# One exponential over two key chunks in a clustered-attention and channel-mix kernel

## The chip, the cores and the metric

The kernel runs on one core of one Trainium2 chip. The metric is device time in microseconds. The kernel before takes 244.97 us (median of 3 runs, 244.86 to 246.22). The profiled execution has a span of 243.7 us from its first to its last instruction.

## The reference

There are 4 batches, 8 heads, 768 positions and 64 values a head. Every query and key is assigned to one of 16 clusters of its head by the largest product with the cluster's normalized centroid, and a query attends only to keys of its own cluster. The attention output, with its heads side by side (512 values a position), goes through a channel mix. All data is fp32 at the ends.

```python
# attention, for each batch and head
mask   = q_assign[:, :, :, None] == k_assign[:, :, None, :]
scores = scale * np.matmul(q, k.transpose(0, 1, 3, 2))
scores = np.where(mask, scores, -1000000000.0)
scores = scores - np.max(scores, axis=-1, keepdims=True)
attn   = np.exp(scores)
attn   = attn / (np.sum(attn, axis=-1, keepdims=True) + 1e-09)
out    = np.matmul(attn, v)
# channel mix; x_prev is x moved on by one position
xk = mu_k * x + (1.0 - mu_k) * x_prev
xr = mu_r * x + (1.0 - mu_r) * x_prev
k  = np.maximum(xk @ w_k, 0.0)          # 512 -> 1024
v  = k * k @ w_v                        # 1024 -> 512
r  = 1.0 / (1.0 + np.exp(-(xr @ w_r)))  # 512 -> 512
return r * v
```

## The kernel before

The heads go in 16 pairs, four to a batch. Queries and keys are transposed, so that the 64 values lie on partitions, and 16 more rows hold each position's cluster as a one-hot vector. The product over these 80 rows gives the score plus a step for "same cluster", which the exponential's bias and scale turn into the mask. The keys come in 6 chunks of 128 (NCH), the queries in thirds of 256 (QT). A *group* is one third of the queries for the two heads of a pair, so it has 6 steps of scores and exponentials, and 4 blocks of value matmuls. There are 48 groups and 288 steps. A column of ones beside the values gives the sum of the exponentials, by which `norm` divides.

The score tiles lie in PSUM, each one bank of 512 columns (two heads by 256 queries), in a ring of four:

```python
ptp   = ctx.enter_context(tc.tile_pool(name="ptp", bufs=3 * NCH))
ps_st = ctx.enter_context(tc.tile_pool(name="ps_st", bufs=4, space=bass.MemoryType.PSUM))

def scores(t):                                    # TensorE, line 315
    g, c = divmod(t, NCH)
    ...
    st = ps_st.tile([128, 2, QT], F32, name="st")
    for s, (tt, hf) in enumerate(parts):
        ...
        nc.tensor.matmul(st[:, s, :].rearrange("p (r u) -> p r u", r=2), w, x, start=True, stop=True)
    sts[t] = st

def exps(t):                                      # ScalarE, line 321
    pt = ptp.tile([128, 2, QT], BF16, name="pt")
    nc.scalar.activation(pt, sts.pop(t), AF.Exp, bias=-BIG, scale=BIG)
    pts[t] = pt

def values(t):                                    # TensorE, line 333: 6 matmuls of 65 columns a block
    ...
    for c in range(NCH):
        nc.tensor.matmul(o[:, i, :], pts[g * NCH + c][:, s, qc * 128:(qc + 1) * 128],
                         vts[n % NR][:, tt, 2 * (c % 3) + c // 3, 0:D + 1], start=(c == 0), stop=(c == NCH - 1))
```

VectorE divides (lines 343, 348), copies the transposed result, and makes the difference to the position before and the two mixes, one for w_k and one for w_r. The first w_k matmul of a batch needs the mix of all four pairs:

```python
def diff(self, n):                                # VectorE, line 401
    ...
    nc.vector.tensor_tensor(self.d, xcur(n, self.hf), xprev(n, self.hf), op=ALU.subtract)
def lerp(self, n, dst, mu):                       # VectorE, line 405: xk and xr
    ...
    nc.vector.scalar_tensor_tensor(out=..., in0=self.d, scalar=mu[:, j:j + 1], in1=xcur(n, self.hf),
                                   op0=ALU.mult, op1=ALU.add)
```

The channel mix is w_k (line 414) into one bank, a Relu on ScalarE (420), a square on VectorE (424), w_r (430) with a Tanh on ScalarE (435), w_v (463), and a product on VectorE (469). For these accumulators there are three banks of their own (`ps_w`); once all attention is done, the score ring and the output bank serve too:

```python
def psum512(pool):
    if pool == "st":
        return ps_st.tile([128, 512], F32, name="mst", tag="st")
    if pool == "o":
        return ps_o.tile([128, 512], F32, name="mo", tag="out2")
    wslot[0] = int(pool[1])
    return wtile([128, 512], F32, "mw")
```

Before a pair's scores, TensorE transposes q and k of the first pairs (line 163, copied by line 173), multiplies by the centroids (195), and VectorE and a hop through DRAM make the one-hot rows (lines 201 to 225).

The order of the instructions on each engine is set when the program is built. Each piece of work is a task with an estimated length, its dependencies, and the ring slots that it takes and frees. The planner runs through these and picks, for each engine, the task that can start first. Tables push single tasks earlier or later (`URGE`, `HOLD`); `PACE0` and `PACE1` set how many score steps go before each slice of channel mix.

```python
task(("scores", t), "PE", 0.225, lambda t=t: scores(t), deps=need, ..., new=[("st", ("st", t))], rank=0, sub=t)
task(("exp", t), "ACT", 0.48, lambda t=t: exps(t), deps=[("scores", t)], uses=[("st", t)],
     new=[("pt", ("pt", t))], rank=1, sub=t)
```

Of the kernel before, what the change touches and what calls it, by code (L numbers as in the profile page):

```python
# [8 lines left out]
F32 = mybir.dt.float32  # L9
BF16 = mybir.dt.bfloat16  # L10
AF = mybir.ActivationFunctionType
# [5 lines left out]
def kernel(  # L17
# [13 lines left out]
    nc = tc.nc  # L31
# [18 lines left out]
    BIG = 32.0  # L50
# [11 lines left out]
    clup = ctx.enter_context(tc.tile_pool(name="clup", bufs=2))  # L62
    ptp = ctx.enter_context(tc.tile_pool(name="ptp", bufs=3 * NCH))
    xnp = ctx.enter_context(tc.tile_pool(name="xnp", bufs=5))
# [5 lines left out]
    hopp = ctx.enter_context(tc.tile_pool(name="hopp", bufs=3, space=bass.MemoryType.DRAM))  # L70
    ps_st = ctx.enter_context(tc.tile_pool(name="ps_st", bufs=4, space=bass.MemoryType.PSUM))
    ps_o = ctx.enter_context(tc.tile_pool(name="ps_o", bufs=1, space=bass.MemoryType.PSUM))
# [228 lines left out]
    def scores(t):  # L301
        g, c = divmod(t, NCH)
        n, parts = groups[g]
        rows = slice(0, 64 + C)
        st = ps_st.tile([128, 2, QT], F32, name="st")
        for s, (tt, hf) in enumerate(parts):
            a = augs[n % NR]
            w = a[rows, 2 + tt, c // (NCH // 2), :]
            if n < ROWS:
                w = w[:, (c % (NCH // 2)) * 128:(c % (NCH // 2) + 1) * 128]  # L310
            else:
                w = w.rearrange("k (u m) -> k m u", m=NCH // 2)[:, c % (NCH // 2), :]
            x = a[rows, tt, 1, hf * QU:(hf + 1) * QU]
            x = bass.AP(tensor=x.tensor, offset=x.offset, ap=[x.ap[0], [-HS, 2], x.ap[-1]])
            nc.tensor.matmul(st[:, s, :].rearrange("p (r u) -> p r u", r=2),  # L315
                             w, x, start=True, stop=True)
        sts[t] = st

    def exps(t):
        pt = ptp.tile([128, 2, QT], BF16, name="pt")  # L320
        nc.scalar.activation(pt, sts.pop(t), AF.Exp, bias=-BIG, scale=BIG)  # L321
        pts[t] = pt

# [57 lines left out]
    def psum512(pool):  # L381
        if pool == "st":
            return ps_st.tile([128, 512], F32, name="mst", tag="st")
        if pool == "o":
            return ps_o.tile([128, 512], F32, name="mo", tag="out2")
        wslot[0] = int(pool[1])
        return wtile([128, 512], F32, "mw")
# [110 lines left out]

    HOLD = {('aff1', 1): 11.7, ('diff', 0, 0): 34.3, ('load', 3, 0): 10.6, ('norm', 12): 70.5, ('xcp', 3, 2): 69.8}
    URGE = {('aff', 6): -1, ('aff1', 1): -1, ('affb', 1): -1, ('affb', 5): -1, ('cast', 1, 2): -1, ('cast', 6, 0): -1, ('cast', 7, 3): -1, ('diff', 1, 1): -1, ('diff', 2, 1): 2, ('hop1', 5): -1, ('hop2', 3): 4, ('lerpk', 0, 0): -1, ('lerpr', 0, 0): -1, ('load', 4, 0): -1, ('load', 5, 1): -1, ('load', 6, 4): 4, ('load', 7, 2): 4, ('load', 8, 1): 4, ('load', 8, 2): -1, ('load', 8, 4): 4, ('load', 8, 5): -1, ('norm', 1): -1, ('norm', 14): 2, ('norm', 3): -1, ('out', 0, 0, 0): 4, ('psk', 0, 0, 0): -1, ('relu', 0, 0, 3): -1, ('scores', 19): -1, ('scores', 21): -1, ('scores', 22): -1, ('scores', 35): -1, ('scores', 38): -1, ('scores', 45): -1, ('scores', 57): 2, ('scores', 63): 4, ('scores', 66): -1, ('scores', 68): -1, ('scores', 75): 4, ('scores', 77): -1, ('scores', 82): -1, ('scores', 90): -1, ('scores', 94): -1, ('scores', 96): -1, ('tcp', 1, 1): -1, ('tcp', 2, 0): -1, ('tpe', 5, 0): -1, ('vcast', 2): -1, ('vcast', 3): -1, ('wv', 0): 2, ('wv', 6): -1, ('xcp', 1, 2): -1, ('xcp', 2, 2): -1, ('xtr', 1, 2): 2, ('xtr', 2, 0): -1, ('xtr', 3, 2): -1}  # L500
    MARGIN = 0.46
    WK, WR, WV = 20.1, 52.3, 35.9
    ROWS = 6
    PACE0, PACE1 = 115.3, 2.13
    PREP = 7
    LATE = {"load": 2.7, "vload": 2.7, "hop1": 0.6, "hop2": 1.0, "xcp": 1.2}
    TAIL = {"PE": 0.25 + MARGIN, "ACT": 0.2 + MARGIN, "DVE": 0.15 + MARGIN, "POOL": 0.15, "SP": 0.0}

# [115 lines left out]
    with tc.manual_schedule():  # L624
# [18 lines left out]
        def use_pe(m):  # L643
            wps = ps_st.tile([128, 512], F32, name="wps", tag="st")
            for i in range(m):
                nc.tensor.matmul(wps[:, 0:256], warm[:, 0:128], warm, start=True, stop=True)  # L646
# [59 lines left out]
        STEPB = NSTEP // B  # L706
        START = {3: 0, 4: 15, 5: 45, 6: 35, 7: 45}
        for n in range(2 * NP, NPAIR):
            b, j = divmod(n, NP)
            START[n] = STEPB * b - 53 + 15 * j  # L710
        moving = {}
# [22 lines left out]
        for n in range(1, NPAIR):  # L734
# [17 lines left out]
            if n > 0:  # L752
                task(("vload", n), "SP", 0.63, lambda n=n: load_v(n, nc.sync), rank=2, sub=due[n] + 4, step=due[n] - 13,
                     new=[("vnat", ("vnat", n))], behind=[("vload", n - 1)] if n > 1 else [])
                moving["vload", n] = 1.1
# [48 lines left out]
        for t in range(NSTEP):  # L804
            g, c = divmod(t, NCH)
            n, parts = groups[g]
            need = sum((ready(n, tt) for tt in {tt for tt, _ in parts}), []) if c == 0 else []
            task(("scores", t), "PE", 0.225, lambda t=t: scores(t), deps=need, after=0.0 if t else 9.9, behind=[("scores", t - 1)] if t else [],
                 new=[("st", ("st", t))], rank=0, sub=t)
            task(("exp", t), "ACT", 0.48, lambda t=t: exps(t), deps=[("scores", t)], uses=[("st", t)],  # L810
                 new=[("pt", ("pt", t))], rank=1, sub=t)
        for t in range(NVAL):
# [3 lines left out]
                 deps=[("exp", g * NCH + NCH - 1), ("vcast", n)] if i == 0 else [],  # L816
                 uses=[("pt", g * NCH + c) for c in range(NCH)] + ([("o", g)] if i else []),
                 new=[] if i else [("o", ("o", g))], rank=2, sub=t)
# [111 lines left out]
        for i in range(4):  # L930
            task(("wk", i), "POOL", 0.75, lambda i=i: load_wk(i), rank=0, after=WK + 3.9 * i)
            moving["wk", i] = 1.8
# [3 lines left out]
        for i in range(4):  # L936
            task(("wv", 2 * i), "POOL", 0.75, lambda i=i: load_wv(2 * i), rank=2, after=WV + 2.4 * i)
            moving["wv", 2 * i] = 1.8

        rings = {"w0": 1, "w1": 1, "w2": 1, "st": 4, "o": 1, "nat": 4, "vnat": 3, "qkT": 2, "t1": 2, "ohn": 2, "oht": 2, "hop": 3,  # L940
                 "pt": 3 * NCH, "xn": 5, "xk": 6, "xr": 6, "k2": 2, "diff": 3, "kr": 3, "tanh": 3, "out": 3}
        held = {"nat": [("nat", i) for i in range(3)], "vnat": [("vnat", 0)], "qkT": [("qkT", 0)]}
# [29 lines left out]
```

The softmax here doesn't subtract the row's maximum and nothing guards it: scores larger than these inputs give would overflow.

## Time and profile before

| | before |
|---|---|
| time, median of 3 | 244.97 us |
| span of the profiled execution | 243.7 us |
| TensorE busy | 237.6 us |
| ScalarE busy | 193.4 us |
| VectorE busy | 190.1 us |
| GpSimd busy | 90.9 us |
| TensorE clock granted | 0.997 |

PE is TensorE's matmuls, PEld its weight loads, DVE VectorE, ACT ScalarE, POOL GpSimd, SP the engine that issues most transfers. The busy tenths cut the span into 40 slices of 6.1 us. In the groups, the columns are line, engine, operation, output and input, count, busy time in us and mean length in ns, and after the second bar the idle time of the engine just before, with what ended it. A matmul's end is modelled, and consecutive ones overlap in the record. The chain of waits follows the work that ended last back to the start, and cuts each piece to the time that it added. In a timeline the columns are the start, the length of the merged run, the engine and the operation with its count. A row by stretch gives for each engine the busy time and, in brackets, its instructions, and then the granted clock, the transfer share and GB/s.

### The profile page before, as it was taken

Reading aid. Unit: us, or ns where it says so; the run is one execution under the profiler, and the core shown is the slowest. Engines: PE = TensorE matmul, PEld = TensorE weight load, DVE = VectorE, ACT = ScalarE, POOL = GpSimd, SP = SyncE. Lnnn points to the kernel's source line nnn. Section 1 sums busy time; section 2 is a strip of 40 time slices with the busy share of each in tenths; the row PEclk is TensorE's granted clock in tenths of the full one; section 3 lists DMA queues with packets and bytes.
Section 4 is the critical chain, followed back from the end, with each engine's and each line's share of the span. In section 5 each row is a group of like instructions: output and inputs, shape, how many; then the busy total and the mean of one; then the engine's idle time right before and its main releaser. Section 6 shows DMA issues by size and latency. Waiting matters only on the chain.

```text
span 243.7 us, 7114 instructions
## 1 busy us (share of the span) xinstructions
PE 237.6 (98%) x2693; PEld 177.3 (73%) x2693; DVE 190.1 (78%) x496; ACT 193.4 (79%) x370; POOL 90.9 (37%) x183
## 2 busy tenths in 40 slices
PE   8999999999999999999999999999999999999994
PEld 6777885878669677876967767867778769576562
DVE  3498899999988989799879897999648577663232
ACT  5279999999889989998988778989987989442340
POOL 3648959476376153313662615355400000000000
PEclk9999999999999999999999999999999999999998
DMA  6955599999999988569795777672622121122112
GB/s 166 312 176 106 137 234 283 193 142 186 133 227 159 175 158 164 109 157 173 164 177 115 157 103 213 108 182 67 169 74 71 29 65 57 29 83 86 46 44 86
DMA packets 94659, 33.61 MB, mean 138 GB/s; under 512 B 75296, under 2 KB 91168, under 8 KB 94624
## 3 DMA queue, kind: packets, MB, share of 16 engines
q1 hardware_dynamic: 91072, 30.19, 56.4%
q0 software_dynamic: 2208, 2.62, 7.1%
q10 hardware_dynamic: 1344, 0.33, 0.7%
q8 instruction: 21, 0.34, 0.7%
q14 instruction: 14, 0.11, 0.2%
HBM read 25.63 MB, written 7.77 MB: 137 GB/s over the span
## 4 chain that ended last, share of the span: by engine, by line
PE 90%; DVE 7%; ACT 1%; issue 1%; ACTq 0%
PE st L315 24%; PE mw L414 15%; PE mw L463 14%; PE out L333 13%; PE mw L430 6%; PE affps L195 4%; PE mst L414 2%; PE mst L463 2%; PE trps L163 2%; PE wps L646 2%; PE mst L430 2%; PE mo L430 1%; DVE xr L405 1%; DVE xk L405 1%; DVE aug L179 1%; DVE qkT L173 1%
## 5 line engine op out<-in xcount | busy, mean ns | idle before, releaser
L321 ACT ACTIVATE pt<-st 128x512 bf16<-128x512 f32 x288 | 151.5, 640 | 12.6 <-PE st L315 11.5
L179 POOL TENSOR_SCALAR aug<-qkT 64x384 bf16<-64x384 f32 x122 | 65.1, 534 | 72.7 <-DVE qkT L153 42.9
L315 PE MATMUL st<-aug 80*128 80x256 bf16 x576 | 91.4, 272 | 0.7
L315 PEld LDWEIGHTS <-aug 80*128 80x128 bf16 x576 | 52.6, 101 | 24.5 <-issue 10.8
L333 PE MATMUL out<-vt,pt 128*128 128x65 bf16 x1152 | 49.1, 192 | 0.0
L333 PEld LDWEIGHTS <-pt 128*128 128x128 bf16 x1152 | 46.1, 97 | 3.1 <-issue 0.6
L414 PE MATMUL mw<-xk,w_k_sb 128*128 128x256 bf16 x336 | 42.6, 272 | 0.0
L414 PEld LDWEIGHTS <-w_k_sb 128*128 128x128 bf16 x384 | 36.9, 98 | 5.1
L463 PE MATMUL mw<-w_v_sb,k 128*128 128x512 bf16 x160 | 40.4, 378 | 0.0
L424 DVE TENSOR_TENSOR k<-kr 128x512 bf16<-128x512 bf16 x48 | 21.9, 455 | 12.5 <-ACT kr L420 12.3
L420 ACT ACTIVATE kr<-mw 128x512 bf16<-128x512 f32 x42 | 25.7, 611 | 7.2 <-PE mw L414 6.8
L463 PEld LDWEIGHTS <-k 128*128 128x128 bf16 x184 | 17.4, 97 | 14.6
L405 DVE SCALAR_TENSOR_TENSOR xr<-diff,mu_r_sb,xt 128x256 bf16<-128x256 bf16 x48 | 24.9, 536 | 0.0
L405 DVE SCALAR_TENSOR_TENSOR xk<-diff,mu_k_sb,xt 128x256 bf16<-128x256 bf16 x48 | 23.2, 503 | 0.1
L153 DVE STREAM_TRANSPOSE qkT<-qk_nat 128x384 f32<-128x384 f32 x40 | 21.8, 557 | 0.2 <-DMA qk_nat<-in_k_dram 0.2
L186 POOL CAST vt<-v_nat 128x384 bf16<-128x384 f32 x32 | 17.5, 576 | 11.5 <-DMA v_nat<-in_v_dram 10.6
L469 DVE SCALAR_TENSOR_TENSOR out_sb<-tanh,mw 128x512 f32<-128x512 bf16 x20 | 13.5, 674 | 10.1 <-PE mw L463 6.9
L348 DVE TENSOR_TENSOR xn<-out,rs 128x256 bf16<-128x256 f32 x46 | 19.5, 424 | 1.6
L401 DVE TENSOR_TENSOR diff<-xt 128x256 bf16<-128x256 bf16 x48 | 16.0, 333 | 1.1
L430 PE MATMUL mw<-w_r_sb,xr 128*128 128x512 bf16 x64 | 16.4, 378 | 0.0
L430 PEld LDWEIGHTS <-xr 128*128 128x128 bf16 x96 | 9.0, 97 | 7.2
L343 DVE RECIPROCAL rs<-out 128x4 f32<-128x4 f32 x48 | 8.2, 171 | 7.1 <-PE out L333 6.6
(70 smaller groups left out, 178.5 us busy)
## 6 DMA issues: line engine op xcount, KB each, us to landing
v_nat<-in_v_dram SPq DMA_DIRECT2D x16, 384.0 KB, 5.2
out_dram<-out_sb SPq DMA_DIRECT2D x23, 256.0 KB, 2.2
qk_nat<-in_q_dram SPq DMA_DIRECT2D x40, 96.0 KB, 3.4
qk_nat<-in_k_dram SPq DMA_DIRECT2D x40, 96.0 KB, 3.6
qk_rows<-in_q_dram SPq DMA_DIRECT2D x5, 384.0 KB, 5.9
qk_rows<-in_k_dram SPq DMA_DIRECT2D x5, 384.0 KB, 6.6
hop<-oht SPq DMA_DIRECT2D x15, 96.0 KB, 2.3
aug<-hop SPq DMA_DIRECT2D x15, 96.0 KB, 3.6
```

Source lines behind the costliest of these rows:

```text
L153: nc.vector.transpose(qkT[n][:, g, :], nat[n][:, g // 2, (g % 2) * GW:(g % 2 + 1) * GW])
L179: (eng or nc.gpsimd).tensor_scalar(augs[n % NR][0:64, g, par, :], in0=qkT[n][64 * par:64 * par + 64, g, :], scalar1=qk_scale, scalar2=1.0, ...
L315: nc.tensor.matmul(st[:, s, :].rearrange("p (r u) -> p r u", r=2), w, x, start=True, stop=True)
L321: nc.scalar.activation(pt, sts.pop(t), AF.Exp, bias=-BIG, scale=BIG)
L333: nc.tensor.matmul(o[:, i, :], pts[g * NCH + c][:, s, qc * 128:(qc + 1) * 128], vts[n % NR][:, tt, 2 * (c % 3) + c // 3, 0:D + 1], start=( ...
L348: nc.vector.tensor_tensor(x.rearrange("p q t d -> p t q d"), o[:, :, 0:D].rearrange("p (t q) d -> p t q d", t=2), rs.rearrange("p (t q) -> ...
L405: nc.vector.scalar_tensor_tensor(out=dst[:, j, :].rearrange("p (r u) -> p r u", r=2), in0=self.d, scalar=mu[:, j:j + 1], in1=xcur(n, self. ...
L414: nc.tensor.matmul(ps[:, i * QT:(i + 1) * QT], w_k_sb[:, j, (2 * i2 + i) * 128:(2 * i2 + i + 1) * 128], self.xk[:, j, :], start=(j == 0), ...
L420: nc.scalar.activation(self.kr[i2], self.ps.pop(i2), AF.Relu, scale=0.5 ** 0.5)
L424: nc.vector.tensor_tensor(self.k2[:, 2 * i2:2 * i2 + 2, :].rearrange("p i u -> p (i u)"), kr, kr, op=ALU.mult)
L430: nc.tensor.matmul(ps, self.xr[:, j, sl], w_r_sb[:, j, :], start=(j == 0), stop=(j == NJ - 1))
L463: nc.tensor.matmul(self.ps["v", c], self.k2[:, i, sl], w_v_sb[:, i, :], start=(i == 0), stop=(i == NI - 1))
```

## The change

Two steps of scores share a tile of two PSUM banks, and one exponential of 1024 columns takes both. This halves the number of exponentials (144 in place of 288), for less fixed cost on ScalarE. The rings keep their bytes: two score tiles of two banks, 9 exponential tiles of twice the size. A value block reads its half of the tile. Where the score ring serves the channel mix, an accumulator takes the first bank of a tile. The planner has new lengths (0.86 for an exponential), and its tables and constants were searched anew, so the order differs on all engines; among others the w_k and w_v loads are placed closer together, and the loads and preparation of later pairs start at other steps.

```diff
-    ptp = ctx.enter_context(tc.tile_pool(name="ptp", bufs=3 * NCH))
+    ptp = ctx.enter_context(tc.tile_pool(name="ptp", bufs=3 * NCH // 2))
-    ps_st = ctx.enter_context(tc.tile_pool(name="ps_st", bufs=4, space=bass.MemoryType.PSUM))
+    ps_st = ctx.enter_context(tc.tile_pool(name="ps_st", bufs=2, space=bass.MemoryType.PSUM))
@@ scores
-        st = ps_st.tile([128, 2, QT], F32, name="st")
+        if t % 2 == 0:
+            sts[t // 2] = ps_st.tile([128, 2, 2, QT], F32, name="st")
+        st = sts[t // 2][:, t % 2]
...
-        sts[t] = st
@@ exps
-        pt = ptp.tile([128, 2, QT], BF16, name="pt")
-        nc.scalar.activation(pt, sts.pop(t), AF.Exp, bias=-BIG, scale=BIG)
-        pts[t] = pt
+        pt = ptp.tile([128, 2, 2, QT], BF16, name="pt")
+        nc.scalar.activation(pt, sts.pop(t // 2), AF.Exp, bias=-BIG, scale=BIG)
+        pts[t - 1], pts[t] = pt[:, 0], pt[:, 1]
@@ psum512
-            return ps_st.tile([128, 512], F32, name="mst", tag="st")
+            return ps_st.tile([128, 2, 512], F32, name="mst", tag="st")[:, 0]
@@ the planner's constants (HOLD and URGE, some 90 entries, left out)
-    MARGIN = 0.46
+    MARGIN = 0.19
-    PACE0, PACE1 = 115.3, 2.13
-    PREP = 7
-    LATE = {"load": 2.7, "vload": 2.7, "hop1": 0.6, "hop2": 1.0, "xcp": 1.2}
+    PACE0, PACE1 = 107.6, 2.16
+    PREP = 13
+    LATE = {"load": 2.7, "vload": 2.7, "hop1": 0.0, "hop2": 1.0, "xcp": 1.2}
@@ when later pairs may be loaded
-        START = {3: 0, 4: 15, 5: 45, 6: 35, 7: 45}
+        START = {3: 0, 4: 15, 5: 45, 6: 50, 7: 52}
-            START[n] = STEPB * b - 53 + 15 * j
+            START[n] = STEPB * b - 75 + 14 * j
@@ tasks
             task(("scores", t), "PE", 0.225, ...
-                 new=[("st", ("st", t))], rank=0, sub=t)
-            task(("exp", t), "ACT", 0.48, lambda t=t: exps(t), deps=[("scores", t)], uses=[("st", t)],
-                 new=[("pt", ("pt", t))], rank=1, sub=t)
+                 new=[] if t % 2 else [("st", ("st", t + 1))], uses=[("st", t)] if t % 2 else [], rank=0, sub=t)
+            if t % 2:
+                task(("exp", t), "ACT", 0.86, lambda t=t: exps(t), deps=[("scores", t - 1), ("scores", t)], uses=[("st", t)],
+                     new=[("pt", ("pt", t))], rank=1, sub=t)
@@ weight loads
-            task(("wk", i), "POOL", 0.75, lambda i=i: load_wk(i), rank=0, after=WK + 3.9 * i)
+            task(("wk", i), "POOL", 0.75, lambda i=i: load_wk(i), rank=0, after=WK + 1.7 * i)
-            task(("wv", 2 * i), "POOL", 0.75, lambda i=i: load_wv(2 * i), rank=2, after=WV + 2.4 * i)
+            task(("wv", 2 * i), "POOL", 0.75, lambda i=i: load_wv(2 * i), rank=2, after=WV + 1.3 * i)
@@ rings
-        rings = {..., "st": 4, ..., "pt": 3 * NCH, ...}
+        rings = {..., "st": 2, ..., "pt": 3 * NCH // 2, ...}
```

## The prediction

> **What bounds the kernel now.** I read the page's busy shares first, then the busy tenths, then the groups by line, the chain of waits in order of time, and last the timelines of ScalarE and VectorE in the stage where the chain leaves TensorE.
>
> ```profile
> PE 237.6 (98%) x2693; PEld 177.3 (73%) x2693; DVE 190.1 (78%) x496; ACT 193.4 (79%) x370; POOL 90.9 (37%) x183
> ...
> PE   8999999999999999999999999999999999999994
> PEld 6777885878669677876967767867778769576562
> DVE  3498899999988989799879897999648577663232
> ACT  5279999999889989998988778989987989442340
> ...
> L321 ACT ACTIVATE pt<-st 128x512 bf16<-128x512 f32 x288 | 151.5, 640 | 12.6 <-PE st L315 11.5
> ...
> L315 PEld LDWEIGHTS <-aug 80*128 80x128 bf16 x576 | 52.6, 101 | 24.5 <-issue 10.8
> ```
>
> Over the whole span the bound is TensorE, at 98%, and the exponential (line 321) belongs to an engine that is busy 79% of the time. But busy matmuls overlap in this record, so 98% does not say that TensorE has only 2% to give. I count its work from the chain, where each piece is cut to the time it added: 8 score matmuls take 0.88 us, 24 value matmuls 0.73, 8 of w_k 0.875, 4 of w_r or w_v 0.86, an affinity block 0.78, 8 transposes of q and k 0.91, 2 of the back transposes 0.11. Times their numbers: scores 576/8 x 0.88 = 63.4; values 1152/24 x 0.73 = 35.0; w_k 384/8 x 0.875 = 42.0; w_r 24 x 0.86 = 20.6; w_v 46 x 0.86 + 1.8 = 41.4; affinities 15 x 0.78 = 11.7; transposes 6.8 + 1.3; the second half of the first head pair's preparation 1.3 + 0.9 = 2.2. Sum 224.4 us. This work stands between 10.8 us, where the first transposes of the body begin, and 240.1 us, where the last matmul ends: 229.3 us. So TensorE loses only some **4.9 us** in the body.
>
> Where? The first w_k matmul starts at 52.16 us. By the program's order 75 score chunks, 40 value blocks, 5 affinities, 15 q/k transpose blocks and 9 back transposes stand before it, with the 2.2 us above: 16.5 + 7.3 + 3.9 + 6.8 + 1.0 + 2.2 = 37.7 us of work in 41.4 us. So **3.7 us** are lost before it and 1.2 after. What limits that first stage is read from three lists. ScalarE's timeline from 24 to 62 us:
>
> ```profile
> 23.41 30.27 ACT L321 ACTIVATE pt<-st 128x512 bf16<-128x512 f32 x61
> 53.36 0.82 ACT L420 ACTIVATE kr<-mw 128x512 bf16<-128x512 f32 x1
> ```
>
> 61 exponentials without a pause: ScalarE is full there. All engines from 18.85 to 53.36 us (busy time of each in that stretch):
>
> ```profile
> 18.85:53.36 34.51, 33.66 (x461) 26.13 (x460) 32.14 (x87) 34.27 (x70) 26.20 (x48) 1.00 0.90 187
> ```
>
> ScalarE 34.27 of 34.51, VectorE 32.14, and most of VectorE's idle time lies before 30 us. And the chain of waits in the same stage, start and length:
>
> ```profile
> 30.38 0.56 PE out L333 x18
> ...
> 31.60 0.62 DVE xk L405
> ...
> 33.41 0.20 DVE xt L374
> ...
> 38.82 0.64 DVE xk L405
> 39.46 0.49 DVE t L201
> ```
>
> From 30.9 us up to the first w_k matmul the chain runs on VectorE, in pieces of which four are shown (the first line is the value matmuls that release it): it makes the four pairs' x, the differences and the mixes that the first w_k matmul needs. Two engines are thus full together in that stage, ScalarE with exponentials and VectorE with the path that the chain names.
>
> **What the Trainium skill says.** "ScalarE: Activation LUTs", section "What ACT_TABLE_LOAD costs": an ACTIVATE takes a fixed part and 0.833 ns a column, and back-to-back ones overlap by about 93 ns. The trace agrees in form: one exponential lasts 603 ns (median), and they follow each other every (30.27 - 0.60)/60 = 0.495 us, so the overlap is 108 ns. "PSUM — Partial Sum Buffer", section "Specifications (TRN2)", gives 8 banks of 512 fp32 columns, so the new score tile is two banks, and two such tiles are the same four banks as before. "Perfetto Trace Analysis", section "Identifying the Most-Contended Engine", says that matmul busy share is no measure of nearness to the limit; here it is 98% while the first stage loses 3.7 of 41.4 us, so the trace agrees. Its section "Optimization Strategy" says that the most contended engine can change over time, as it does here at about 52 us.
>
> **The change part by part.**
>
> 1. *One exponential in place of two.* An estimate with the skill's slope: 603 + 512 x 0.833 = 1030 ns long, following each other every 1030 - 108 = 922 ns. Two old ones take 990 ns. Gain 68 ns a pair (93 ns if the overlap is the skill's). Over 144 pairs 9.8 us of ScalarE time; its busy time falls from 193 to about 183 us. Nearly all of this lies beside TensorE work. Only the stage to 52 us can feel it: some 35 pairs x 0.068 = **2.4 us** of ScalarE time there.
>
> 2. *Does that stage become 2.4 us shorter?* Only where VectorE lets it. In program order VectorE has about 31.4 us of work from the first transposed affinity to the first mix of the fourth pair in the new kernel, against 31.7 in the old (counts by the pieces of the chain: lerp 0.44, copy of q/k 0.60, norm 0.42 and 0.10, and so on), for which it now takes 51.1 - 15.7 = 35.4 us. So its own work shrinks by 0.3, and its waits and stretched pieces there, 3.7 us, are what can be won. Some of them wait for ScalarE or follow it; I take a third, 1.2 us.
>
> 3. *The ring becomes coarser.* Four tiles of a bank become two of two banks. A tile is refilled only after its exponential of 1.03 us has ended. I lay the new order of TensorE instructions end to end with the pieces above and take the work between the end of a tile's filling and the next filling of that tile. The tile needs 1.03 us and, an estimate from gaps of 0.1 to 0.3 us between scores and exponential in the timeline, about 0.15 more. In the first stage 10 of 31 such gaps are shorter than 1.18, by 3.0 us in all; in the old order (four tiles, 0.60 us) one gap is, by 0.1 us. Most of it falls on time that TensorE lost already, since ScalarE was full; I charge **+0.5 us**. After the first w_k matmul the shortest new gap is 1.58 us and the mean 2.3: with a Relu or Tanh of 0.5 us ahead of the exponential 1.68 is needed, so there is next to no cost there, 0 to 1 us.
>
> 4. *The new order.* The work before the first w_k matmul is 71 score chunks and 42 value blocks in place of 75 and 40, 37.3 us in place of 37.7. The rest is the same instructions, and TensorE's sum of 224.4 us does not change. I charge nothing for it.
>
> 5. *The end.* The mixing stage borrows score tiles as accumulators; two remain in place of four, one bank of each unused. With three others and the output one it has six. From 206 us TensorE works without a gap with eight; each is held for its own 0.87 to 1.73 us and one evacuation of 0.6 to 0.7 us. Six are enough: 0.
>
> Sum: -0.3 - 1.2 + 0.5 = -1.0 us, on 244.97: **244.0 us**.
>
> **Rivals.** (a) *ScalarE is the true limit of the first stage and the chain's VectorE part only runs along with it.* For: 61 exponentials in a row, 34.27 of 34.51 us. Against: the chain names VectorE from 30.9 us on. Then all 2.4 us come back, and with the shorter work 0.4 more: about 242.2. (b) *The coarse ring.* For: the 10 short gaps, and that TensorE and ScalarE are nearly equal in that stage, so either one's wait is the other's. Against: later gaps are long. If the 3.0 us are paid in full and the rest wins nothing: about 247. (c) *Nothing moves*, because TensorE's 224.4 us and the path through VectorE are untouched: 245. (d) *The new order removes nearly all of the 4.9 us lost*: 240 to 241. It would take no idle time at all in a stage with three full engines; I hold it unlikely.
>
> **Range and chances.** The floor is 244.97 - 4.9 = 240.1, which is just the 2% line (240.07), so "faster by over 2%" needs more than everything that I count as lost: 0.04. The other line is 249.9, 4.9 us above; it needs the short gaps in full and stalls in the later stage as well: 0.05. Within 2%: 0.91. Eight times in ten between 241.3 and 247.0: rival (a) with a luckier order below, rival (b) above.
>
> **What would show it.** Step 1: exponentials near 1.03 us, following each other every 0.92 us, ScalarE busy about 183 us. Step 2: the chain between 30 us and the first w_k matmul is still VectorE's, and that matmul starts at 51, not at 49; if it starts before 49.5, rival (a) or (d) was right. Step 3: in the first stage TensorE's score matmuls or weight loads wait for exponentials, some 0.5 us each, and ScalarE's run of exponentials has gaps; the last w_k to w_v stages are without gaps. Step 5: no idle TensorE after 206 us. I would be wrong if the later stage, dense before, showed stalls of TensorE behind exponentials, or if the time fell below 241.

## The result and the profile after

The changed kernel takes 248.19 us (median of 4, 247.59 to 249.42), the kernel before beside it 245.59 us. The ratio is 1.0113, with a 95% interval from 1.0068 to 1.0157: some 2.8 us slower by the ratio, 2.6 by the medians. Predicted were 244.0 us and at most 247.0.

The page of the changed kernel, the parts that answer to those shown of before:

```profile
span 245.8 us, 6877 instructions
...
PE 237.8 (97%) x2693; PEld 178.4 (73%) x2693; DVE 190.2 (77%) x496; ACT 184.5 (75%) x226; POOL 90.9 (37%) x183
...
PE   8999889999999999999999999999999999999994
PEld 6887576877687769777868776966678779676562
DVE  3399899999878969789979899898746477784332
ACT  5279599987789889988965988898797969342340
...
L322 ACT ACTIVATE pt<-st 128x1024 bf16<-128x1024 f32 x144 | 142.7, 1028 | 18.8 <-PE st L317 17.2
...
L317 PE MATMUL st<-aug 80*128 80x256 bf16 x576 | 85.7, 272 | 2.7 <-ACT pt L322 2.3
```

ScalarE's busy time fell from 193.4 to 184.5 us, as it was meant to. But its idle time in front of exponentials rose from 12.6 to 18.8 us, and TensorE's score matmuls now wait for exponentials, which the page of before did not show. In the busy tenths, PE's fifth and sixth slices and ACT's fifth slice have sunk: the loss lies before 55 us. The first w_k matmul starts at 53.4 us, where it was 52.0 in before (the chain of before placed the piece that it added at 52.16). With the prediction's own count, 37.3 us of TensorE work stand between the first transposes at 10.9 us and that matmul, so 5.2 us are lost there; counted to 52.0, before lost 3.5 (3.7 to the chain's 52.16). The last matmul ends at 242.1 us, so the body loses 242.1 - 10.9 - 224.4 = 6.8 us in place of 4.9.

The chain of waits of the changed kernel, from 10 to 62 us (start and length):

```profile
20.22 0.49 DVE oht L216
20.73 1.62 DMA hop<-oht
...
22.42 4.73 DMA aug<-hop
...
27.20 1.05 PE st L317 x8
```

Here is something that the kernel before did not have in its chain. Pair 1's one-hot rows leave VectorE at 20.7 us, go to memory and come back into the score operand at 27.15 us, and the scores of pair 1 start right behind. In before the same two transfers were issued at 19.28 and 20.97 us, and the second landed after 3.6 us, at 24.6. ScalarE's timeline shows a hole of 2.65 us ahead of these scores, where before had none (its first line is the run of four from which step 1 is measured below):

```profile
18.83 3.77 ACT L322 ACTIVATE pt<-st 128x1024 bf16<-128x1024 f32 x4 [0.39 <-PE st L317]
...
24.60 0.59 ACT L171 COPY qkT<-trps 128x512 f32<-128x512 f32 x1
27.85 4.81 ACT L322 ACTIVATE pt<-st 128x1024 bf16<-128x1024 f32 x5 [2.65 <-PE st L317]
32.84 6.64 ACT L322 ACTIVATE pt<-st 128x1024 bf16<-128x1024 f32 x7 [0.18 <-PE st L317]
```

In this profile the late rows are only a small part of the hole. TensorE and its weight loads in the same time:

```profile
23.02 0.60 PE L317 MATMUL st<-aug 80*128 80x256 bf16 x4
23.46 0.89 PE L334 MATMUL out<-vt,pt 128*128 128x65 bf16 x24
24.28 1.82 PE L195 MATMUL affps<-qkT,cblk 128*32 128x384 f32 x8
25.25 0.15 PEld L195 LDWEIGHTS affps<-qkT,cblk 128*32 128x32 f32 x6 [0.83 <-ACT qkT L171]
26.03 0.28 PE L371 MATMUL xtps<-identb,xn 128*128 128x128 bf16 x2
26.15 0.71 PE L334 MATMUL out<-vt,pt 128*128 128x65 bf16 x18
27.20 1.05 PE L317 MATMUL st<-aug 80*128 80x256 bf16 x8 [0.34 <-DMA aug<-hop]
```

Between the last scores of pair 0, which start at 23.35 us, and the first of pair 1 the new order puts 42 value matmuls, an affinity block (the product with the centroids, line 195) and two back transposes; in before these two scores are 0.66 us apart. TensorE waits for the rows for only 0.34 us. The affinity block takes 1.82 us where before's took 0.85, because ScalarE copies part of its q and k (line 171) only at 24.60 us, behind exponentials; the record counts this stall as busy.

### The profile page after: what moved, and what is told of

It is laid out like the page before. It is cut to its first block, busy times and chain, and to the rows that moved or that the text cites. A ratio compares the mean times of both kernels' runs of the same rounds, so it can differ in the third digit from the quotient of the medians.

```text
span 245.8 us, 6877 instructions
## 1 busy us (share of the span) xinstructions
PE 237.8 (97%) x2693; PEld 178.4 (73%) x2693; DVE 190.2 (77%) x496; ACT 184.5 (75%) x226; POOL 90.9 (37%) x183
## 4 chain that ended last, share of the span: by engine, by line
PE 79%; DVE 12%; DMA 5%; POOL 1%; issue 1%; ACT 0%; SPq 0%
PE st L317 20%; PE mw L464 15%; PE mw L415 14%; PE out L334 11%; PE mw L431 7%; PE affps L195 3%; DMA w_r_sb<-in_moe_w_r_dram 2%; DVE qkT L173 2%; DMA aug<-hop 2%; PE wps L647 2%; DVE xk L406 1%; PE mst L415 1%; PE mst L464 1%; DVE xr L406 1%; POOL aug L179 1%; DVE diff L402 1%
## 5 line engine op out<-in xcount | busy, mean ns | idle before, releaser
L322 ACT ACTIVATE pt<-st 128x1024 bf16<-128x1024 f32 x144 | 142.7, 1028 | 18.8 <-PE st L317 17.2
L179 POOL TENSOR_SCALAR aug<-qkT 64x384 bf16<-64x384 f32 x122 | 66.4, 545 | 81.0 <-DVE qkT L153 49.4
L317 PE MATMUL st<-aug 80*128 80x256 bf16 x576 | 85.7, 272 | 2.7 <-ACT pt L322 2.3
L317 PEld LDWEIGHTS <-aug 80*128 80x128 bf16 x576 | 54.6, 101 | 23.7 <-issue 9.8
L464 PE MATMUL mw<-w_v_sb,k 128*128 128x512 bf16 x168 | 42.3, 378 | 0.0
L470 DVE SCALAR_TENSOR_TENSOR out_sb<-tanh,mw 128x512 f32<-128x512 bf16 x21 | 14.4, 685 | 11.8 <-PE mw L464 11.1
L406 DVE SCALAR_TENSOR_TENSOR xr<-diff,mu_r_sb,xt 128x256 bf16<-128x256 bf16 x48 | 22.9, 496 | 0.0
L186 POOL CAST vt<-v_nat 128x384 bf16<-128x384 f32 x32 | 16.3, 538 | 11.3 <-DMA v_nat<-in_v_dram 10.6
L431 PE MATMUL mw<-w_r_sb,xr 128*128 128x512 bf16 x76 | 19.7, 378 | 0.3 <-DMA w_r_sb<-in_moe_w_r_dram 0.3
L436 ACT ACTIVATE tanh<-mw 128x512 bf16<-128x512 f32 x19 | 11.4, 603 | 6.6 <-PE mw L431 6.6
```

Of the source, the lines that this page charges most:

```text
L179: (eng or nc.gpsimd).tensor_scalar(augs[n % NR][0:64, g, par, :], in0=qkT[n][64 * par:64 * par + 64, g, :], scalar1=qk_scale, scalar2=1.0, ...
L322: nc.scalar.activation(pt, sts.pop(t // 2), AF.Exp, bias=-BIG, scale=BIG)
L406: nc.vector.scalar_tensor_tensor(out=dst[:, j, :].rearrange("p (r u) -> p r u", r=2), in0=self.d, scalar=mu[:, j:j + 1], in1=xcur(n, self. ...
L431: nc.tensor.matmul(ps, self.xr[:, j, sl], w_r_sb[:, j, :], start=(j == 0), stop=(j == NJ - 1))
L464: nc.tensor.matmul(self.ps["v", c], self.k2[:, i, sl], w_v_sb[:, i, :], start=(i == 0), stop=(i == NI - 1))
```

## The experiments

Two theories were put against each other. Theory R: the ring is too coarse; scores wait for the long exponential of their tile. Theory O: the new order costs by itself, through the late one-hot rows or elsewhere. A ratio is always to the kernel before, run beside it on the same chip; the number in brackets is its 95% interval. Before's own runs with a lowered clock are left out of the ratios, while most such runs of the other kernels are in, so where it matters the median of the runs with a mean granted clock of 0.997 or more ("at full clock") is given too, against before's at full clock. The kernel of one move was measured twice on one chip and gave 1.0018 and 1.0046, so I call differences below 0.3% unresolved.

**The old order with merged exponentials.** Instructions stay where before had them; two steps share a tile, and the exponential stands at the odd step.

```diff
+        if t % 2 == 0:
+            sts[t // 2] = ps_st.tile([128, 2, 2, QT], F32, name="st")     # ring of 2
+        st = sts[t // 2][:, t % 2]
...
     def exps(t):
+        if t % 2 == 0:
+            return
+        pt = ptp.tile([128, 2, 2, QT], BF16, name="pt")
+        nc.scalar.activation(pt, sts.pop(t // 2), AF.Exp, bias=-BIG, scale=BIG)
...
```

> The order of before on every engine, with the paired score tiles and the exponential of 1024 columns put in at the places of the odd steps: the structural half of the change alone. Theory R (the coarse ring costs: scores wait for the one long exponential of their tile): slower than before by 1 to 4 us, 246.5 to 249.5, with waits of TensorE's score matmuls for exponentials before 55 us. Theory O (the new order costs: the first one-hot rows come back late, work stands in a worse order): within 1 us of before, 244.5 to 246.5, since ScalarE has less to do and nothing else is moved.

Measured: 254.79 us, ratio 1.0354 [1.0311, 1.0397]. The change without its new order costs 9 us, far more than theory R had asked for.

**The same, with two exponentials at their old places:** the ring alone.

```diff
+        if t % 2 == 0:
+            pair[0] = ptp.tile([128, 2, 2, QT], BF16, name="pt")
+        pts[t] = pair[0][:, t % 2]
+        nc.scalar.activation(pts[t], sts[t // 2][:, t % 2], AF.Exp, bias=-BIG, scale=BIG)
```

> The old order with two score tiles of two banks, but two exponentials of 512 columns, each at its old place: the ring alone, without the merging. The merged kernel on this order took 254.8 us, 8.9 more than before. Theory R1 (the tile size does it: a bank is free again only when both halves have been read): 250 to 255. Theory R2 (the merging does it: the first half's exponential starts only when the second half's scores are there, and nothing of the tile is free for 1.03 us): within 2 us of before, 245 to 248.

Measured: 258.14 us, ratio 1.0520 [1.0491, 1.0549]. So it is the tile's size, not the merging, and the merging wins back 3 to 4 us (258.14 against 254.79; 0.0166 of the ratio) of what the ring loses. The lists of waits, first of the merged one, then of this one (us in all, times, longest):

```profile
PE st L317 <- ACT pt L324: 6.2, 18, 0.9
```

```profile
PE st L317 <- ACT pt L326: 10.2, 27, 0.7
```

and of the changed kernel, with its own order:

```profile
PE st L317 <- ACT pt L322: 2.3, 7, 0.5
```

The searched order takes away most of these waits. After 55 us it takes away all: there the changed kernel's list has no wait of scores for exponentials, and the merged old order has this:

```profile
PE st L317 <- ACT pt L324: 2.8, 7, 0.9
```

**The old tables, planned anew** for the new tiles (the edit against the changed kernel):

```diff
-    MARGIN = 0.19
+    MARGIN = 0.46
...
-    PACE0, PACE1 = 107.6, 2.16
-    PREP = 13
+    PACE0, PACE1 = 115.3, 2.13
+    PREP = 7
...
-        START = {3: 0, 4: 15, 5: 45, 6: 50, 7: 52}
+        START = {3: 0, 4: 15, 5: 45, 6: 35, 7: 45}
```

The rest of the tables (`HOLD`, `URGE`, `LATE`) and the spacing of the loads go back to before's in the same way.

> The changed tiles and exponentials, planned anew by the planner (which knows the ring of two), but with the constants and tables of before: no search. It shows how much of the ring's cost the planner and how much the search took away: the old order itself took 254.8. If the ring's cost is inherent to the first stage, 249 to 255 even when planned for it; if planning for the ring is enough, 246 to 248.5 and the new tables won little.

Measured: 256.57 us, 1.0442 [1.0395, 1.0488]. The median says too much: four of its six runs had a clock of 0.985 to 0.993, and the two at full clock took 251.98 and 254.05, which is 6.4 and 8.5 us above before's 245.55. The planner alone, though it knows the ring, does not remove the cost. The changed kernel at full clock is 1.9 to 2.2 us above before (below), so the searched constants and tables are worth some 4 to 6.5 us. In its profile the first w_k matmul comes 39.6 us after the first score matmul (40.3 in before, 42.0 in the changed kernel), but only 132 score matmuls stand ahead of it, against 150 and 142, so that is no quicker stage. From there to the end it needs 199.7 us, against 191.7 and 192.4.

**The new order with old tiles and two exponentials:**

```diff
-            sts[t // 2] = ps_st.tile([128, 2, 2, QT], F32, name="st")     # ring of 2
+        st = sts[t] = ps_st.tile([128, 2, QT], F32, name="st")            # ring of 4
...
+        for h in range(2):
+            nc.scalar.activation(pt[:, h], sts.pop(t - 1 + h), AF.Exp, bias=-BIG, scale=BIG)
```

> The order of the changed kernel, but four score tiles of one bank and two exponentials of 512 columns: the order half of the change alone. Theory R: the waits of scores for exponentials (2.3 us in seven waits) go, and the time comes back to before's or under it, 244.5 to 246. Theory O: it stays at 247.5 to 249.

Measured: 248.37 us, 1.0089 [1.0067, 1.0112]. Ten of its 22 runs had a lowered clock; the twelve at full clock have a median of 247.23, 1.6 us above before's 245.66. Theory O stands: with before's tiles and exponentials the new order alone is slower than before. The waits of scores for exponentials are gone, and the time is not.

**The changed kernel with two exponentials of 512 columns:**

```diff
-        nc.scalar.activation(pt, sts.pop(t // 2), AF.Exp, bias=-BIG, scale=BIG)
+        st = sts.pop(t // 2)
+        for h in range(2):
+            nc.scalar.activation(pt[:, h], st[:, h], AF.Exp, bias=-BIG, scale=BIG)
```

> The changed kernel with each exponential split into two of 512 columns again; tiles, ring and order stay as changed. It shows what the saved fixed cost is worth on this order. If ScalarE's length of work matters in the first stage (both theories allow it): each pair takes 0.07 us more, some 33 pairs before the first w_k matmul, so up to 2.3 us slower than the changed kernel, 249 to 250.5. If ScalarE has slack because it waits anyway: within 0.7 us of the changed kernel, 247.5 to 249.

Measured: 249.52 us, 1.0140 [1.0081, 1.0199]. That lies in the first expectation, but three of its six runs had a lowered clock; the median of the three at full clock, 248.06, lies in the second. It is not resolved from the changed kernel.

**The late rows: one swap on VectorE.** The back transpose of pair 1's one-hot rows goes ahead of the first division; nothing else moves.

```diff
+            elif k.key == ("norm", 0):
+                tasks["affb", 1].fn()
+                k.fn()
+            elif k.key != ("affb", 1):
                 k.fn()
```

> The changed kernel with one swap on VectorE: the back transpose of pair 1's one-hot rows goes ahead of the first group's division (0.7 to 1 us earlier), so the hop through memory starts earlier. Theory O: the scores of pair 1, which waited for these rows at 27.2 us after ScalarE had stood idle for 2.65 us, start 0.5 to 1.5 us earlier and the time falls by 0.5 to 1.5 us, to 246.7 to 247.7. Theory R: the start moves but the end does not, as the stage is held by the ring and VectorE: within 0.4 us of the changed kernel.

Measured: 246.60 us, 1.0018 [0.9998, 1.0038]; by the medians at full clock 0.9 us above before. None of its 22 runs had a lowered clock. In its profile ScalarE's hole is still 2.45 us.

**The changed kernel again,** as control:

> The changed kernel once more, unaltered, on the chip of the three runs sent with it: the reference for small differences, since the start of the body moved by 1.0 us between profiles (first score matmuls at 11.4 and at 10.4 us). Every theory: 247 to 249. If it lies at 246.6, the swap of the run before had no effect and its lower time was the chip's.

Measured: 249.49 us, 1.0170 [1.0141, 1.0199]. Six of its seven runs had a mean granted clock of 0.993 and took 248.9 to 250.2 us; the seventh, at 1.0, took 247.5.

**One swap in the transfer queue.** Pair 1's rows return ahead of the load of pair 4's queries.

```diff
+            elif k.key == ("load", 4, 0):
+                tasks["hop2", 1].fn()
+                k.fn()
+            elif k.key != ("hop2", 1):
                 k.fn()
```

> The changed kernel with one swap in the transfer queue: the one-hot rows of pair 1 go back into the score operand before the 384 KB load of pair 4's queries is issued, not behind it. Theory O (queue order delays pair 1's rows, which took 4.7 us to land, against 3.6 to 4.1 in the kernel before): they land in about 4 us, scores of pair 1 start 0.5 to 0.9 us earlier, time 0.4 to 0.9 us under the control. Theory R: the stage is held by ring and VectorE, no change within 0.3 us.

Measured on the control's chip: 247.00 us, 1.0069 [1.0045, 1.0092], clear of the control's interval and more than expected. The rows landed after 4.0 us, in the control's profile after 5.3. None of its 11 runs had a clock under 0.997, so part of the win is the clock (below). Against the control's one run at full clock, 247.5, it is 0.5 us, which is what the earlier landing should give, but one run does not settle it.

**Three moves together,** the two above and the second w_r load issued with the first:

```diff
...
+            elif k.key == ("wr", 0):
+                k.fn()
+                tasks["wr", 2].fn()
+            elif k.key in (("affb", 1), ("wr", 2), ("hop2", 1)):
+                pass
...
```

> The changed kernel with three small moves together: the back transpose of pair 1's one-hot rows ahead of the first division, these rows' return ahead of the load of pair 4's queries, and both w_r loads issued at 44 us instead of 44 and 54 (a w_r matmul waited 0.3 us for the second at 60 us). Theory O: what each won adds up: 1 to 2.5 us under the control, 245.5 to 247. If it is under before (245.9 by the last runs) by more than 0.6 us, the change is a gain with these moves. Theory R: no more than 0.5 us under the control.

Measured: 247.03 us, 1.0060 [1.0037, 1.0083]: no more than the swap alone. The late w_r load, though the chain runs through it, is worth nothing that shows.

**The opposite swap in the kernel before:**

```diff
...
+            elif k.key == ("hop2", 1) and tasks["load", 4, 0].end is None:
+                tasks["load", 4, 0].fn()
+                k.fn()
+            elif k.key == ("load", 4, 0):
+                pass
```

> The kernel before with the opposite swap alone: pair 4's queries (384 KB) are loaded ahead of the return of pair 1's one-hot rows. Theory O says that this place in the queue is worth 2 us wherever the rows are the next thing TensorE needs: 1.5 to 2.5 us slower than before, 247 to 248. If pair 1's rows had slack in the old order: within 0.7 us of before.

Measured: 245.83 us, 1.0010 [0.9996, 1.0024]; the rows landed after 4.4 us instead of 3.6. Theory O's number fails here: in the old order they had nearly enough slack (TensorE waited 0.41 us for them), because they left VectorE earlier. The place in the queue costs only where it meets rows that are already late.

**The queue swap with the old tiles, and with the coarse ring and two exponentials.** The edits are those shown above, combined:

```diff
+                tasks["hop2", 1].fn()         # both: ahead of ("load", 4, 0)
+            nc.scalar.activation(pt[:, h], sts.pop(t - 1 + h), AF.Exp, bias=-BIG, scale=BIG)   # first: ring of 4
+            nc.scalar.activation(pt[:, h], st[:, h], AF.Exp, bias=-BIG, scale=BIG)             # second: ring of 2
```

> The changed kernel's order with the queue swap (one-hot rows of pair 1 ahead of pair 4's queries), and four score tiles of one bank with two exponentials of 512 columns. If the rest of the loss is the ring's waits net of what the merging saves: at or under before, 244.5 to 246 (ratio 0.996 to 1.003). If the searched order costs in other places too: 246 to 248, no better than the swapped changed kernel at 247.0.

Measured: 246.88 us, 1.0048 [1.0032, 1.0065].

> As that, but with the coarse ring of two tiles and two exponentials of 512 columns. Against the swapped changed kernel (247.0, ratio 1.007) it shows what the merging saves: by 0.07 to 0.1 us for each of some 33 pairs of the first stage 2 to 3 us if ScalarE bounds it (249 to 250), nothing to 1 us if not (247 to 248). Against the fine ring of the run beside it, it shows what the ring costs on this order: 1 to 3 us expected, as 10 of 31 gaps were too short by 3.0 us.

Measured beside it: 247.55 us, 1.0082 [1.0056, 1.0107]. The difference, 0.7 us, is what the ring costs on this order; it is less than expected, and the intervals overlap a little. The merged form with the swap (1.0069, on another chip) lies between the two. In the list of waits of the old tiles with the swap, ScalarE's idle time behind scores is halved (17.2 us in the changed kernel):

```profile
ACT pt L321 <- PE st L315: 8.9, 22, 2.0
```

The longest of these waits is the hole ahead of pair 1. It stays at 2.0 us although TensorE no longer waits for the rows, so it belongs to the order:

```profile
26.17 23.10 ACT L321 ACTIVATE pt<-st 128x512 bf16<-128x512 f32 x46 [2.00 <-PE st L315]
```

**The moves apart and together, on one chip.** The edits are again those above: both moves with the old tiles, the unaltered changed kernel, the VectorE move alone, both moves.

```diff
+            elif k.key == ("norm", 0):        # first, third and fourth
+                tasks["affb", 1].fn()
+                k.fn()
+            elif k.key == ("load", 4, 0):     # first and fourth
+                tasks["hop2", 1].fn()
+                k.fn()
```

> The new order with both moves (back transpose of pair 1's rows ahead of the first division, and their return ahead of pair 4's queries), with four tiles of one bank and two exponentials of 512 columns. If the late rows are all that the new order costs: within 0.5 us of before (ratio 0.998 to 1.002). If the order costs elsewhere too: 1.003 to 1.006, as with one move (1.0048).

> The changed kernel, unaltered, beside the runs sent with it: ratio 1.010 to 1.018 to before.

> The changed kernel with the back transpose of pair 1's rows first (0.6 us earlier) and the queue as it was. If the place in the queue is what costs: 1.008 to 1.016, little under the unaltered one. If the earlier start is worth as much as the run on another chip said (1.0018): 1.000 to 1.004.

> The changed kernel with both moves. If they add up: 1.000 to 1.004. If the swap in the queue already removed the late landings and the stage is then held by VectorE and the ring: 1.005 to 1.008, as with the swap alone (1.0069).

Measured: 246.90 us, 1.0044 [1.0027, 1.0062] with the old tiles; 247.82 us, 1.0077 [1.0046, 1.0108] unaltered; 246.64 us, 1.0046 [1.0030, 1.0063] with one move; 247.03 us, 1.0066 [1.0042, 1.0091] with both. The moves do not add up, and on this chip their win is within the intervals. At full clock the four are 1.3, 2.1, 1.1 and 1.4 us above before. Even with early rows and the old tiles some 1.1 to 1.3 us of the new order's loss remain.

Where does it lie? The profiles of the two kernels with old tiles and early rows lose 4.6 and 5.0 us of TensorE time before the first w_k matmul, those of the two kernels in the old order with old tiles (before, and before with the opposite swap) 3.5 and 4.0; behind it 2.1 in both, against 1.4 and 2.5. As far as single profiles tell, it is in the first stage. What differs there is the affinity block that waits for ScalarE's copy. All 15 profiles of the new order have this stall, of 0.7 to 1.0 us, the one with both moves and old tiles too; none of the five others has it:

```profile
23.27 1.73 PE L195 MATMUL affps<-qkT,cblk 128*32 128x384 f32 x8
24.15 0.15 PEld L195 LDWEIGHTS affps<-qkT,cblk 128*32 128x32 f32 x6 [0.74 <-ACT qkT L171]
```

Its size fits, but no run moved that copy, so this is a candidate and not shown.

**Is the clock part of it?** The profile of the unaltered kernel in that set fell on a run with a lowered clock. Its row by stretch (busy time by engine in the order PE, PEld, DVE, ACT, POOL; the third figure from the right is the granted clock):

```profile
26.00:28.00 2.00, 0.93 (x13) 0.73 (x10) 1.19 (x4) 0.15 (x1) 1.81 (x4) 1.00 1.06 247
...
30.00:32.00 2.00, 2.00 (x11) 1.75 (x11) 1.93 (x9) 0.89 (x2) 1.29 (x2) 0.50 1.12 213
```

and the first scores of pair 1 in the same profile:

```profile
27.20 1.05 PE L317 MATMUL st<-aug 80*128 80x256 bf16 x8 [1.07 <-DMA aug<-hop]
```

The clock falls to half at 29.2 us and rises again 3.4 us later; TensorE was idle for half of 26 to 28 us. PE's 2.00 at 30 to 32 us is the trap in this view: it is full, with 11 matmuls, where the first profile of the changed kernel, at full clock, has 26 in that stretch. Seven profiles have such a wait: at 1.07, 1.28 and 1.59 us the clock fell, at 0.34, 0.41, 0.62 and 0.89 us it did not. The last pair of runs was to test the cause by filling the wait.

```diff
+        if t == 3 * NCH:                       # pair 1's first scores
+            for i in range(10):
+                nc.tensor.matmul(st[:, 0, :], warm[:, 0:128], warm, start=True, stop=True)
```

> The changed kernel with ten matmuls of 256 columns on a constant tile (1.1 us of work, overwritten and used by nothing) ahead of pair 1's first scores, where TensorE waits 0.3 to 1.3 us for the one-hot rows. If TensorE's idle time there is what lowers its clock: the mean granted clock is 0.997 or more in all runs, and the time lies at 247 to 248, though up to 1 us of work is added. If the clock has another cause: runs at 0.993 stay as frequent as in the unaltered kernel beside it, and the time is the same or up to 1 us longer.

> The changed kernel, unaltered, on the same chip. Of its runs so far 11 of 23 had a mean granted clock of 0.993 and took 248.4 to 250.2; the others took 246.3 to 248.8. Expected: a mixture of both again, median 247.7 to 249.5.

Measured: 247.35 us, 1.0086 [1.0058, 1.0114] filled, all runs at 0.997 or more; 246.94 us, 1.0065 [1.0032, 1.0099] unaltered, all at 0.999 or more. The control did not fall either, so this tells nothing of the cause. It does show what the changed kernel takes at full clock on this chip: 1.9 us more than before (245.04).

Two things on record say more. On the two chips that had both kinds, 22 of 47 runs of the new order without a move had a clock below 0.997, and 2 of 100 with a move. The moves do little but bring the rows earlier, so it is the late rows that bring the lowered clock. And in every profile the stretches between two changes of the clock are whole multiples of 3.413 us: in the three with a fall before 50 us it was up for 23.89 us, 7 times as long, and then down for 3.41. With each profile cut from the rise into windows of this length, the windows that end at the three falls hold 1.57, 1.84 and 2.19 us of busy TensorE. Of the 1,320 other windows between 10 and 235 us only one comes as low, with 2.19 us in the control's profile, and its clock did not fall; the next holds 2.29. Here are the row of the unaltered kernel whose clock fell and that of the control:

```profile
25.82:29.23 3.41, 1.84 (x28) 1.51 (x25) 2.10 (x8) 1.38 (x2) 3.10 (x6) 1.00 0.80 179
24.94:28.35 3.41, 2.19 (x37) 1.76 (x35) 2.02 (x6) 0.91 (x1) 3.10 (x6) 1.00 1.09 240
```

So it fits that idle time within one such window lowers the clock, and that the same wait is harmless where a boundary cuts it in two. No run tests this by itself.

## Why the prediction was wrong

**Step 1, the exponential, was right.** Predicted 1030 ns, measured 1028. Four in a row took 3.77 us, so they follow each other every (3.77 - 1.02)/3 = 0.917 us (predicted 0.922). ScalarE's busy time is 184.5 us (about 183).

**Step 2 failed.** It said that the first stage would win back 0.3 us of work and 1.2 us, "a third", of VectorE's waits and stretched pieces. It was the reverse: the first w_k matmul came at 53.4 us and not at 51. One reason is a misread chain. "Up to the first w_k matmul the chain runs on VectorE" is wrong; in before it leaves VectorE 9.6 us earlier:

```profile
42.05 0.42 DVE xn L348
42.55 0.27 PE xtps L370 x2
...
52.16 0.88 PE mw L414 x8
```

From 42.55 us TensorE's own work is the chain, so the "waits and stretched pieces" counted up to 51.1 us were not all there to be won. The other reason is the start. In the changed kernel the chain does stay on VectorE from 28 to 50 us, but it starts late, because it first waits for pair 1's rows. I took time off a path without having looked at what feeds its start: in the new order of VectorE the first division stands ahead of the back transpose, and in the queue a 384 KB load stands ahead of the rows' return. Both were in the order of instructions that I had read.

**Step 3 was right in mechanism and close in size.** Counted were 10 gaps too short by 3.0 us before the first w_k matmul and none behind it; the profile has seven waits of 2.3 us, all before 53 us. Charged were 0.5 us; on this order the ring measured 0.7 (0.0034 of a ratio, with intervals that overlap); what the merging gives back of that is not resolved. On the old order the ring alone costs 12.7 us, which I had not priced.

**Step 4 is the one that decided.** "I charge nothing for it" was the wrong term. The new order with the old tiles measured 1.0089 [1.0067, 1.0112], 2.2 us, or 1.6 us at full clock; with the queue swap, or both moves, 1.0048 and 1.0044, about 1.1 us. So the new order lost time in two places of its first stage: the late rows of pair 1, and, with these out of the way, about 1.1 us more, for which the stalled affinity block is the candidate. Why the new order is poorer stays open. My reading, which no run shows, is that an order searched for a harder ring gives up places that the old order could choose freely; that the search just ended at a poorer order is as possible. The prediction took "searched anew" for "no worse".

**Step 5 was right:** neither TensorE's matmuls nor its weight loads show a wait after 206 us.

**The sum.** At full clock the changed kernel is 1.9 to 2.2 us above before (one run of 247.49, and medians of 247.68 and 246.94, beside 245.34, 245.55 and 245.04). In place of -0.3 - 1.2 + 0.5 this is about 1.3 us of order apart from the late rows (246.86 with both moves and old tiles, beside 245.55), and some 0.6 to 0.9 us for the late rows and for the ring net of the saved fixed cost, which the runs do not tell apart (the ring net: 1.0066 against 1.0044 with both moves, unresolved). On top comes the lowered clock in some runs, about 2 us in the control (a median of 249.5 in six runs, 247.49 in one). Of the rivals, (b) named the ring with 247 us; on this order the ring's own waits are not the main cost, and that it forced the order is not shown.

**Open:** whether the stalled affinity block is the last 1.1 us of the order, and whether idle TensorE is what lowered its clock when the rows were late. No version measured here beats the kernel before; the nearest, the changed kernel with the back transpose first, took 246.60 and 246.64 us beside 245.88 and 245.68.

## What to carry to other kernels

Merging two evacuations saves a fixed cost, but it also halves the number of tiles in the ring, and where the evacuating engine is the limit, the stage that could gain is also the one where a coarse ring hurts most. Price the ring with the old order first, by the work that stands between a tile's filling and its next filling; if the order has to be rebuilt for it, charge the rebuilt order as a cost of the change. When an order changes, follow the first thing that each stage needs (here a 96 KB return behind a 384 KB load, and a copy of q and k behind exponentials) before taking time off the stage.

## What the runs showed of the hardware

The return of 96 KB landed 4.4 to 5.9 us after its issue in ten profiles where a 384 KB load had been issued just ahead of it, and 3.6 to 4.2 us where that load came behind. A matmul's busy time hides a lowered clock, and a stall inside a block: at a granted 0.50, 2 us of "full" TensorE held 11 matmuls, and eight affinity matmuls lasted 1.82 us instead of 0.85 without a gap in the record. The granted clock changed only at whole multiples of 3.413 us from its last change; it fell for 3.41 us in three profiles, after TensorE waits of 1.07 to 1.59 us, and in four with waits of 0.34 to 0.89 us it did not. That the wait itself was the cause is not shown; that runs with earlier rows hardly have it (2 of 100 against 22 of 47) is.
